# Pooled attention and a residual MLP: casting loads for the first batches, TensorE pools v and k, and a new order of the head

## The chip, the cores and the metric

The kernel runs on one NeuronCore of a Trainium2 chip. TensorE (PE) multiplies matrices, VectorE (DVE) and ScalarE (ACT) work on vectors and may read PSUM, GpSimd (POOL) works on vectors in SBUF and issues the DMAs that cast while they load, SyncE (SP) issues the other DMAs. Each engine runs its instructions in the order in which they were emitted and waits on semaphores where it needs another engine's result. The metric is the time of one execution on the device in microseconds (us), and less is better.

## What is computed

There are 8 batches, 8 heads, 576 positions, 64 features per head.

```
k_p = mean of k over groups of 8 positions     # 72 rows per head
v_p = mean of v over groups of 8 positions
attn = softmax(q @ k_p.T / 8)                  # 576 x 72 per head
x = attn @ v_p, heads side by side             # 8 x 576 x 512
a1 = alpha1 * x + beta1
u = x + lam * (w_tok @ a1)                     # mixes the 576 positions
out = u + lam * (relu((alpha2 * u + beta2) @ w_ch1) @ w_ch2)   # 512 -> 2048 -> 512
```

Inputs and output are fp32; the matmuls take bf16 and fp16.

## The kernel before

The 576 positions of a batch are cut into chunks of 128: four whole ones, and the last 64 positions of two batches share a fifth. The 36 chunks are taken in blocks of four, so there are nine blocks. For each block the kernel runs an MLP: part A (`mlp_A`, L479) multiplies w1 with four chunks of u, 16 steps j of 4 matmuls of 512 columns, each evicted by ScalarE with a relu into a tile `Hj`; part B (`mlp_B`, L497) multiplies `Hj` with w2 in four chunks of four parts.

The attention of a batch b is made of small pieces. `att_F` (L321) turns q to the layout that the scores need, four TensorE transposes and one copy for each pair of heads, or one crossbar transpose on a DMA queue for b > 1. `att_Frem` does so for the last 64 positions. `att_K` (L350, L353) pools k: a matmul with a mask `pool_main` sums positions, after `sum_k` on POOL (L133, L135) has added each four neighbours into one; the result goes to `kpT` in two copies. `att_V` (L364, L366) pools v by three additions on VectorE. `att_S` (L376, L379) makes the scores of one head, three matmuls and two exponentials on ScalarE into a tile `ET`. `att_AV` (L395 to L403) multiplies with v and divides by the sum (the ones stand in a column of the tile `vp1`). `att_X` (L410, L414) multiplies with lam and alpha1 into `xs`. `mix_T` (L444) mixes the positions of one chunk with w_tok, VectorE adds x, and `mix_uT` (L458, L463) turns the result for the MLP. `cast_rem` casts and sums the last 64 positions of q and k.

The order is written out by hand (`manual_schedule`). Ahead of the first MLP step stands a straight list: loads, constants, the attention of batch 0, w_tok's transposes and row sums (L249, L261), four mixes, and the first MLP steps. This is called the head. After it, each block n sorts a list of pieces by a number written beside each: step j of part A has j, parts of B have 16 to 31, and the pieces of the attention of batch n + 1 have numbers between. The function `attention` gives these numbers. An engine's queue has its instructions in that order, DMA issues included: SP's queue holds the loads of q (fp32, batches 0 and 1), k, v and the remainders, the crossbar transposes and the stores; POOL's queue holds the casting loads of w_tok, w1, w2 and, from batch 2 on, q. A tile that a pool hands out again makes the next writer wait for the last reader: `k_raw`, `q_raw`, `v_u` have two buffers each, PSUM's `gp` has six.

In the head of the kernel before, POOL issues the small vectors, then builds the masks by selections, sums k of batch 0, issues w_tok, w1 and w2. VectorE fills the constants in the first 4.7 us, then casts q, waits for beta (L519) and runs on. `keep_warm` (L434) issues matmuls whose result nobody reads.

## Time and profile before

| | before |
|---|---|
| median of 4 runs | 370.61 us (369.58 to 371.78) |
| the profiled execution | 370.36 us |
| its span in the trace | 368.7 us |
| TensorE / VectorE / ScalarE / POOL busy | 94% / 62% / 42% / 22% of the span |
| read from HBM, written to it | 38.04 MB, 9.44 MB |

The profile is one execution. Its page gives for each engine the busy time and the number of instructions, and rows of 40 digits, each the busy share of a fortieth of the span in tenths. PEclk is the clock that the throttle granted to TensorE, in tenths. A row of the stage table is: the stretch in us, its length, busy time and number of instructions of PE, PE's weight loads, DVE, ACT, POOL, then granted clock, busy share of the DMA engines, GB/s. A row of waits is: who waited for whom, total us, times, the longest. A row of the timeline is: start, length, engine, line, operation, out<-in with the form, how many in a row, and in brackets the idle time before it with what ended it.

### The profile page before, as it was taken

The page shows a single profiled execution, that of the slowest core. Times are in us where ns is not written, and L with a number is a line of the kernel's source. Part 1 is how long each engine was busy: PE and PEld are TensorE (multiplying, and loading weights), DVE is VectorE, ACT ScalarE, POOL GpSimd, SP SyncE. Part 2 cuts the span into 40 slices and gives each one's busy share as a digit, 9 for nine tenths or more (in the row PEclk, how much of TensorE's full clock was granted, in tenths as well). Part 3 has the DMA queues.
Part 4 walks back from the last instruction along what each step waited for, and adds up shares of the span by engine and source line. Part 5 has one row for each costly group of instructions (what it writes and reads, how often), then busy time and mean ns, then how long its engine had stood idle before and what let it go on. Part 6 is the DMA issues. An engine that isn't in the chain of part 4 may idle for free.

```text
span 368.7 us, 5783 instructions
## 1 busy us (share of the span) xinstructions
PE 347.8 (94%) x2179; PEld 188.3 (51%) x2179; DVE 228.1 (62%) x459; ACT 156.5 (42%) x317; POOL 82.7 (22%) x94
## 2 busy tenths in 40 slices
PE   2889999789999999999999999999999999999994
PEld 0466656445654565456545654565456545544541
DVE  4697927898876587758775887587748871011011
ACT  1674657316830483048303830384038403703700
POOL 7554143760003500350044003400330000000000
PEclk9999999999999999999999999999999999999999
DMA  8999997937726792788287737864730032011011
GB/s 199 231 186 213 262 196 172 173 46 189 145 72 185 146 164 65 179 183 153 75 212 143 135 75 215 153 132 81 212 80 2 24 92 71 2 57 57 2 57 57
DMA packets 63931, 46.93 MB, mean 127 GB/s; under 512 B 31448, under 2 KB 54044, under 8 KB 63904
## 3 DMA queue, kind: packets, MB, share of 16 engines
q1 hardware_dynamic: 54496, 38.55, 44.7%
q0 software_dynamic: 9408, 8.02, 14.6%
q8 instruction: 17, 0.28, 0.3%
q14 instruction: 10, 0.08, 0.1%
HBM read 38.04 MB, written 9.44 MB: 129 GB/s over the span
## 4 chain that ended last, share of the span: by engine, by line
PE 87%; DVE 7%; DMA 2%; issue 1%; POOL 1%; ACT 0%; POOLq 0%; DVEq 0%
PE ps_h L479 34%; PE ps_ch L497 33%; PE ps_tok L444 12%; PE ps_sc L376 3%; DMA vecs<-in_moe_beta_dram 2%; PE ps_av L395 2%; DVE v_u L364 2%; DVE x_tm L403 2%; DVE xs L410 1%; PE ps_sc L379 1%; DVE vp L366 1%; DVE xs L414 1%; PE ps_uT L463 1%; PE ps_bias L302 1%; DVE rec L401 0%
## 5 line engine op out<-in xcount | busy, mean ns | idle before, releaser
L484 ACT ACTIVATE Hj<-ps_h,bias_cols 128x512 bf16<-128x512 f32 x144 | 98.5, 687 | 154.9 <-PE ps_h L479 153.8
L479 PE MATMUL ps_h<-u_fm,w 128*128 128x512 bf16 (+2 forms) x592 | 137.3, 374 | 0.0
L497 PE MATMUL ps_ch<-w,Hj 128*128 128x512 bf16 x576 | 134.7, 379 | 0.0
L497 PEld LDWEIGHTS <-Hj 128*128 128x128 bf16 x576 | 55.0, 98 | 61.6
L479 PEld LDWEIGHTS <-w 128*128 128x128 bf16 x592 | 62.6, 114 | 45.0 <-issue 0.3
L502 DVE TENSOR_TENSOR u_sb<-u_sb,ps_ch 128x512 f32<-128x512 f32 x36 | 24.6, 687 | 73.8 <-PE ps_ch L497 73.4
L444 PE MATMUL ps_tok<-xs,wtT 128*128 128x512 bf16 (+1 forms) x200 | 49.6, 379 | 3.4 <-DVE xs L410 3.2
L381 ACT ACTIVATE ET<-ps_sc 72x256 f16<-72x256 f32 (+1 forms) x128 | 44.5, 402 | 5.5 <-PE ps_sc L376 4.2
L446 DVE TENSOR_TENSOR u_sb<-x_tm,ps_tok 128x512 f32<-128x512 f32 (+1 forms) x40 | 27.5, 687 | 23.1 <-PE ps_tok L444 23.1
L364 DVE TENSOR_TENSOR v_u<-v_u 72x512 f32<-72x512 f32 x64 | 36.3, 567 | 2.7 <-DMA v_u<-in_v_dram 1.1
L403 DVE TENSOR_TENSOR x_tm<-ps_av,rec 128x320 f32<-128x320 f32 x64 | 31.5, 492 | 2.3
L444 PEld LDWEIGHTS <-wtT 128*128 128x128 bf16 (+1 forms) x200 | 19.1, 98 | 26.5 <-issue 3.7
L118 POOL CAST rem_q<-rem_raw 128x256 bf16<-128x256 f32 x7 | 3.0, 431 | 131.2 <-DMA rem_raw<-in_q_dram 131.2
L448 DVE TENSOR_TENSOR u_bf<-u_sb,al_bc 128x512 bf16<-128x512 f32 (+1 forms) x38 | 29.6, 779 | 1.7 <-DMA u_fm<-u_bf 0.3
L376 PE MATMUL ps_sc<-qT,kpT 128*72 128x256 bf16 x128 | 26.7, 291 | 2.2 <-ACT kpT L358 1.2
L133 POOL TENSOR_TENSOR k_raw<-k_raw 128x512 f32<-128x512 f32 x16 | 20.9, 1304 | 20.9 <-DMA k_raw<-in_k_dram 19.0
L395 PEld LDWEIGHTS <-ET 72*128 72x128 f16 x256 | 16.5, 102 | 12.2 <-DVE v_u L364 0.8
L410 DVE TENSOR_TENSOR xs<-x_tm,lamal_bc 128x512 bf16<-128x512 f32 x29 | 22.0, 759 | 0.9
L135 POOL TENSOR_TENSOR k_bf<-k_raw 128x512 bf16<-128x512 f32 x16 | 22.1, 1382 | 1.3
L401 DVE RECIPROCAL rec<-ps_av 128x5 f32<-128x5 f32 x64 | 12.3, 192 | 15.2 <-PE ps_av L399 14.3
L395 PE MATMUL ps_av<-vp,ET 72*128 72x66 f16 x256 | 18.6, 199 | 0.4 <-ACT ET L381 0.4
L358 DVE CAST kpT<-ps_kp 64x288 bf16<-64x288 f32 x28 | 12.7, 455 | 7.5 <-PE ps_kp L353 7.1
(98 smaller groups left out, 207.4 us busy)
## 6 DMA issues: line engine op xcount, KB each, us to landing
k_raw<-in_k_dram SPq DMA_DIRECT2D x16, 512.0 KB
v_u<-in_v_dram SPq DMA_DIRECT2D x16, 512.0 KB
out_dram<-u_sb SPq DMA_DIRECT2D x32, 256.0 KB
w<-in_moe_w_ch_dram POOLq DMA_DIRECT2D x8, 512.0 KB, 13.7
q_bf<-in_q_dram POOLq DMA_DIRECT2D x12, 256.0 KB, 5.2
q_raw<-in_q_dram SPq DMA_DIRECT2D x4, 512.0 KB
rem_raw<-in_q_dram SPq DMA_DIRECT2D x16, 64.0 KB
rem_raw<-in_k_dram SPq DMA_DIRECT2D x16, 64.0 KB
```

The costliest lines, as they stand in the source:

```text
L364: nc.vector.tensor_tensor(out=t[:, :, 0:n], in0=t[:, :, 0:n], in1=t[:, :, n:2 * n], op=ALU.add)
L376: nc.tensor.matmul(out=ps_sc[0:SPG, 0:256], lhsT=kpT_pool[u][:, half, h % 4, :], rhs=st["qT"][u][:, 2 * (h % 4):2 * (h % 4) + 2, :])
L381: nc.scalar.activation(out=ET[:, n0:n0 + n], in_=ps_sc[0:SPG, 0:n], func=AF.Exp, bias=0.0, scale=0.125)
L395: nc.tensor.matmul(out=av[:, c, :], lhsT=ET[:, m0:m0 + 128], rhs=vp1[:, hh, :])
L403: nc.vector.tensor_tensor(out=x[:, :, dd:dd + D], in0=av[:, :, 0:64], in1=rec.unsqueeze(2).to_broadcast((P, 5, D)), op=ALU.mult)
L410: eng.tensor_tensor(out=xs[:, 0:4, cols], in0=x[:, 0:4, cols], in1=lamal_bc[:, cols].unsqueeze(1).to_broadcast((P, 4, D * (h1 - h0))), op= ...
L444: nc.tensor.matmul(out=ps_tok, lhsT=wtT[0:kk, at, t0:t0 + P], rhs=xs[0:kk, sc, :], start=(sc == 0), stop=(sc == 4))
L446: nc.vector.tensor_tensor(out=s["u"][p0:p1, :], in0=st1[b]["x"][p0:p1, c, :], in1=ps_tok[p0:p1, 0:DM], op=ALU.add)
L448: eng.tensor_tensor(out=s["u_bf"][p0:p1, :], in0=s["u"][p0:p1, :], in1=al2_bc[p0:p1, :], op=ALU.mult)
L479: nc.tensor.matmul(out=ps_h[:, t0:t1], lhsT=w1_of(cc, j), rhs=u_fm[n][:, cc, t0:t1], start=(cc == 0), stop=(cc == 3))
L484: nc.scalar.activation(out=t, in_=ps_h, func=AF.Relu, bias=bias_cols[:, j:j + 1], scale=1.0)
L497: nc.tensor.matmul(out=ps, lhsT=Hj[n, j][:, 128 * m:128 * m + 128], rhs=w2[j // 4][:, j % 4, :], start=(j == 0), stop=(j == NJ - 1))
```

## The change

The head is rewritten, and the attention of batch 1 takes other ways and other numbers.

- q and k of batch 0, v of batches 0 and 1, and q of batch 1 are loaded by POOL's queue with a cast (`load_q_bf`, `load_k16`, `load_v16`). The small vectors are issued by ScalarE. The order in POOL's queue is: q, k of the first four heads, q, k of the others, v, w_tok, w1, q of batch 1, one part of w2, v of batch 1, the rest of w2, with masks, two `att_X` and two `u_bf` between.
- For batch 0, `sum_k` is gone: `att_K` sums over the four neighbours in PSUM by four matmuls instead of one for each head (a fifth column of k, a copy of the first made by VectorE, lets each matmul take two neighbouring columns), and two instead of one for the remainders. Its two copies are on ScalarE and VectorE.
- For batches 0 and 1, v is pooled by TensorE: `first_V`, six matmuls of 256 columns with masks `pool_v`, `pool_vr` for four heads, and two copies.
- q of batch 1 and three chunks of u go through the crossbar on SP's queue.
- `ET` has eight tiles instead of four.
- Several constants (`more_constants`) are filled in the midst of batch 0's attention and not at the start.
- In block 0 the pieces of batch 1 come earlier, during part A, and the four scalings of w2 (2.29 us each in the trace) are spread over the block.

The core of the diff; lines "..." mark what is left out:

```diff
+    def load_k16(b, u):
+        t = work.tile([P, 4, 5, D], BF, tag="k_raw", bufs=2, name="k16")
+        nc.gpsimd.dma_start(out=t[:, :, 0:4].rearrange("p h c d -> p h (c d)"), in_=rows(k, b, u))
+        st1[b]["k"][u] = t
...
+    def load_v16(b, parts=(0, 1, 2)):
+        if 0 in parts:
+            t = work.tile([P, 6, H, D], F16, tag="v_u", bufs=2, name="v16")
...
+                nc.gpsimd.dma_start(
+                    out=main[:, 4 * u:4 * u + 4].rearrange("p h c d -> p h (c d)"),
+                    in_=rows(v, b, u))
...
+    new_batch(0)
+    load_rem(0)
+    load_q_bf(0, 0)
+    load_k16(0, 0)
+    load_vector(1, moe_alpha1)
+    load_vector(0, moe_lam)
...
+    load_q_bf(0, 1)
...
+    load_k16(0, 1)
+    load_v16(0)
...
+    load_wtok()
...
+    def more_constants():
+        nc.vector.memset(ones_bf, 1.0)
+        nc.vector.memset(ones_lo[0:64], 1.0)
+        nc.vector.memset(ones_lo[64:128], 0.0)
+        nc.vector.memset(warm, 0.0)
+        nc.vector.memset(xs_pool[1][0:64, 4, :], 0.0)
+        nc.vector.memset(wtT[:, :, S:640], 0.0)
+        for i, p0 in ((0, 64), (1, 0)):
+            nc.vector.tensor_tensor(out=xs_pool[i][p0:p0 + 1, 4, :], in0=vecs[p0:p0 + 1, 3],
+                                    in1=vecs[p0:p0 + 1, 0], op=ALU.mult)
...
+        n, nr = (1, 1) if b else (4, 2)
+        if not b:
+            nc.vector.tensor_copy(out=st["k"][u][:, :, 4], in_=st["k"][u][:, :, 0])
         for h in range(4):
-            nc.tensor.matmul(out=kp[:, h, 0:64],
-                             lhsT=st["k"][u][:, h].rearrange("p a d -> p (a d)"), rhs=pool_main)
+            for c in range(n):
+                nc.tensor.matmul(
+                    out=kp[:, h, 0:64],
+                    lhsT=st["k"][u][:, h, c:c + 2].rearrange("p a d -> p (a d)"),
+                    rhs=pool_main, start=(c == 0), stop=(c == n - 1))
...
+    def first_V(b, u, copy=nc.vector.tensor_copy):
...
+        for c in range(4):
+            nc.tensor.matmul(out=vp, lhsT=pool_v, rhs=main[:, heads, c], start=(c == 0), stop=False)
+        for c in range(2):
+            nc.tensor.matmul(out=vp, lhsT=pool_vr, rhs=rest[:, heads, c], start=False,
+                             stop=(c == 1))
+        for r in range(2):
+            copy(out=vp1_pool[2 * u + r][:, :, 0:64],
+                 in_=vp[:, 128 * r:128 * r + 128].rearrange("p (h d) -> p h d", h=2))
...
-        if key[0] > 1:
+        if key[0] > 1 or key in ((1, 0), (1, 1), (0, 4)):
             nc.sync.dma_start_transpose(out=u_fm[blk][:, :, 128 * at:128 * at + 128],
...
+    broadcast(0, lam_bc)
     att_F(0, 0)
+    att_F(0, 1, nc.vector.tensor_copy)
+    cast_rem(0, nc.vector)
+    att_K(0, 0, None)
+    att_Frem(0, nc.scalar.copy)
+    att_S(0, 0)
+    att_S(0, 1)
+    att_F(0, 2, nc.vector.tensor_copy)
+    att_F(0, 3, nc.vector.tensor_copy)
+    att_S(0, 2)
+    att_K(0, 1, None)
     nc.vector.tensor_tensor(out=lamal_bc, in0=lamal_bc, in1=lam_bc, op=ALU.mult)
+    more_constants()
+    att_S(0, 3)
+    att_S(0, 4)
+    first_V(0, 0)
+    att_AV(0, 0)
+    att_S(0, 5)
+    att_AV(0, 1)
+    for g in range(4):
+        load_w1(g)
+    att_X(0, 0, 2, nc.gpsimd)
+    first_V(0, 1)
...
+    load_q_bf(1, 0)
+    load_q_bf(1, 1)
+    att_X(0, 2, 4, nc.gpsimd)
+    load_w2(0)
...
+    for u in range(2):
+        load_k(1, u, nc.vector)
+    load_rem(1, behind=nc.vector)
...
     mix_T(0, 1, nc.gpsimd)
+    load_v16(1)
+    for g in range(1, 4):
+        load_w2(g)
...
+        if first:
+            todo.append((3.3, lambda: att_F(b, 0)))
+            todo.append((3.4, lambda: att_F(b, 2)))
+            todo.append((3.5, lambda: cast_rem(b, nc.gpsimd)))
+            todo.append((6.0, lambda: att_Frem(b)))
...
+            todo.append((3.6 + 0.1 * u if first else -0.9 + 1.2 * u,
+                         lambda u=u: sum_k(b, u, nc.gpsimd)))
+            todo.append((6.4 + 3.0 * u if first else 4.1 + 2.0 * u,
+                         lambda u=u: att_K(b, u, nc.scalar.copy if first else nc.vector.tensor_copy)))
+            if first:
+                todo.append((10.2 + 1.4 * u, lambda u=u: first_V(b, u, nc.scalar.copy)))
         for h in range(8):
-            at = 17.0 + 0.9 * h if late else 7.4 + 1.15 * h
-            lag = 1.6 if late else 2.0
+            at = 8.8 + 1.1 * h if first else 7.4 + 1.15 * h
+            lag = 3.0 if first else 2.0
...
-            at = 26.2 + 0.9 * c if late else 19.1 + 1.3 * c
+            at = 21.4 + 1.2 * c if first else 19.1 + 1.3 * c
...
-                todo.append((4.2 + 1.7 * g, lambda g=g: scale_w2(g)))
+                todo.append(((8.0, 13.0, 20.3, 23.9)[g], lambda g=g: scale_w2(g)))
```

## The prediction

> **What bounds the kernel now.** I read the page's shares and 40 slices first, then busy time by stage, then TensorE's waits, then the timeline where stages begin.

> ```profile
> PE 347.8 (94%) x2179; PEld 188.3 (51%) x2179; DVE 228.1 (62%) x459; ACT 156.5 (42%) x317; POOL 82.7 (22%) x94
> ...
> DMA  8999997937726792788287737864730032011011
> ```

> ```profile
> 37.50:56.70 19.20, 18.37 (x168) 11.75 (x168) 11.46 (x11) 12.34 (x24) 6.41 (x6) 1.00 1.06 226
> 56.70:74.70 18.00, 14.41 (x124) 8.52 (x122) 15.31 (x32) 8.35 (x22) 10.89 (x13) 1.00 0.87 163
> 74.70:86.00 11.30, 11.08 (x66) 5.35 (x67) 10.51 (x14) 2.34 (x4) 5.08 (x5) 1.00 0.48 93
> 123.10:160.20 37.10, 37.10 (x231) 19.83 (x229) 27.16 (x54) 15.38 (x32) 8.36 (x10) 1.00 0.70 141
> ```

> ```profile
> PE ps_bc L231 <- DMA vecs<-in_moe_alpha_dram: 7.2, 1, 7.2
> PE ps_tok L444 <- DVE xs L410: 3.2, 2, 2.7
> PE ps_qr L339 <- DVE rem_q L118: 1.4, 1, 1.4
> ```

> ```profile
> 14.71 0.84 PE L376 MATMUL ps_sc<-qT,kpT 128*72 128x256 bf16 x2 [0.48 <-ACT kpT L358]
> ...
> 28.34 0.74 PE L249 MATMUL ps_w<-identity_bf,wt_bf 128*128 128x128 bf16 x5
> ...
> 29.22 0.44 PE L249 MATMUL ps_w<-identity_bf,wt_bf 128*128 128x128 bf16 x5
> ...
> 30.15 1.25 PE L444 MATMUL ps_tok<-xs,wtT 128*128 128x512 bf16 x5 [0.49 <-DVE xs L410]
> ...
> 37.52 0.81 PE L479 MATMUL ps_h<-u_fm,w 128*128 128x384 bf16 x4
> ...
> 85.94 4.26 PE L479 MATMUL ps_h<-u_fm,w 128*128 128x512 bf16 x19
> ```

> From 86 us on TensorE has no gap (37.10 busy of 37.10 in one whole block), and the change leaves that list of work as it is. So all that can change is the start of block 1's first matmul, 85.94. Before it lie two stages: the head, to the first mixing matmul (30.15) and the first MLP matmul (37.52, 7.4 later), and block 0, 48.4 us, of which TensorE idles 0.83 + 3.59 + 0.22 = 4.6. The DMA row is at 9 for the first 64 us: the head is fed by full queues.

> **The loads.** Removed: q, k, v of the first batch as fp32 on SP, and with them q's casts (0.7 on VectorE, 1.1 on ScalarE). Added: as bf16/f16 casts on POOL. In the trace's packet records an fp32 load passes at 340 packets of 1024 B per us (512 packets: 1.5 us); the cast loads of later batches (q_bf) at 380 of 512 B (1.35 us), 2.2 to 2.9 us after POOL begins to issue, and about 1 us more until a waiter runs. Halved bytes thus save a tenth, not half. [...]
> With POOL's first issue at 0.8: q0 usable 5.8, k0 7.1, q1 8.5, k1 9.8, v0 11.2, v1 13.0, w_tok 16.9 (37 packets/us: 3.5 us, and the rest 0.4), w1 19.5 to 27.3 (2.6 each). Before, w_tok ends near 21 and w1 near 31. Each POOL issue costs 0.6 to 0.8 us; q1, k1 and v are issued between the mask selections and still queue behind flowing data, so that is hidden. [...] The small vectors move to ScalarE's queue: one landing took 7.2 us to TensorE's first work, now some 3.5; hidden behind q0.

> **The head, step by step.** F transposes: 8 at 0.107 = 0.9, to 6.7. VectorE then copies qT (0.55), casts rem_q (0.28) and rem_k (two pieces, some 0.4) and fills k's fifth column (bounds 0.1 and 0.3 by the rem_q row; 0.15): 8.1. K's fourth matmul waits for that column; everything on TensorE is queued behind it. The rest of K, 13 of 64 columns at 0.054 and the remainder, ends 9.0 (K now costs 1.0 instead of 0.4 us, twice). kpT: VectorE's half waits for ScalarE's half by their common tile, so 0.4 + 0.4 still: 10.0. The first scores are complete at 10.4 against some 15.2: 4.8 gained, since no POOL sums (2.5) and no DMA of beta through VectorE's queue (the 1.4 wait at L339) are ahead of them.
> Then S1 0.5, F 0.9, S2 0.5, K1 1.0 (with its column): 13.4; kpT of the second half 14.5. Here VectorE's own list comes: lamal 0.68, six memsets (rows 0.11 to 0.27: 1.2), two xs rows 1.3 (L519 took 1.8 with POOL beside; 0.65 each is the lower end, and POOL is idle here), first_V's two copies (no row; half the width of kpT's 0.45 to all of it, 0.2 to 0.45; 0.25): 18.2. TensorE has S3, S4 and V (1.0 + 1.3) done at 15.8 and waits 2.3 us in AV0, everything else queued behind. This is a new wait: the memsets lay under the loads before.
> From 18.2 VectorE leads: eight AV pairs at 0.62 (L401 and L403 by their starts), two copies 0.5, a wait for the second V 0.6, X(4,6) 0.8 and 0.5 for POOL's X beside it (L410 took 0.68 alone, 0.93 and more beside POOL), memsets 0.2, X(6,8) 0.7: 8.3, the mix at 26.5. If TensorE is still at its slow rate, its list from AV0 (8 AV 0.28, 3 S 0.5, V 1.3, broadcast 1.2, 10 transposes 1.1) is 7.4 plus 1.7 for the last AV's X and some VectorE lag: 27.7. Against it stands v's old sums, 6 to 7 us on VectorE in 14.8 to 26.5, gone.
> Which rate? The two L249 rows above are one and the same work at 0.107 and 0.056 us per transpose: TensorE doubled at 29.0, while PEclk says 1.00 throughout. [...] I take 27.0: 3.1 gained. The 7.4 to the first MLP matmul stay (same lists; w1's first part landed by 19.5): 34.4.

> **Block 0.** TensorE loses 18 transposes of q (some 1.1) and three u tiles (0.2 each, now on the crossbar), gains two V (0.7 each): -0.3. Of the 4.6 us idle, 2.7 is L444 waiting for xs behind VectorE and POOL, both full in 56.7 to 74.7 (v sums, k sums, X); the v sums (1.4 x 4) and kpT copies leave VectorE, scores come during the A part, and X has room. What is late next: ScalarE. Between A8 and A15 it has 8 Hj 5.5, 16 ET some 6, kpT and vp 1.8: 13.3 against TensorE's 12.5 (eight A 6.9, S 2.4, V 1.4, K and bias 1.0, AV 0.8), so 1 to 2 us of waits for PSUM. POOL: two u_bf (to 32), six issues (4.5), rem 1.1, sums 2.6 each: k ready at 40.4 and 43, needed by K at 34.4 + 9.5 = 43.9 (four A's 3.7, bias 0.6, three A's 2.6, w_tok's last part with its wait 1.4, the mix of chunk 4 1.2). q's crossbar transposes (1.3 each on SP) wait for q of the second batch (31 to 33), needed near 47; behind them on SP stand only loads for the third batch; v 38, needed 49; w2 40 to 46, needed from 57. All are covered by 3 us or more, and if one is not, TensorE stops in the A part with everything behind it, us for us. The four extra ET memsets (0.11 each) lie under the first load; the extra ET buffers spare waits that the waits of before do not show, so I count nothing. Left idle 2.0: block 43.8 - 0.3 + 2.0 = 45.5, 2.9 gained.

> **Sum.** The profiled run took 370.36 (span 368.7 and 1.7 around it; the median is 370.61): 370.36 - 3.1 - 2.9 = 364.4.

> **Rivals.** (1) As summed, 364.4, own range 361 to 366.5 (fast clock early and no idle in block 0: 370.4 - 4.5 - 4.6): 0.60. (2) Only one half comes: VectorE's chain or ScalarE in block 0 eats it. For: both run at 95% there. Time 370.4 - 3.1 = 367.3: 0.20. (3) It does not do what it says: POOL's first load is as late as the vectors' 6.3 us to landing (2 us), VectorE's list adds 1, block 0 idles as before: 370: 0.12. (4) Slower: the clock gate. The new waits at K, K1 and AV0 keep the rate slow past the mix. From the mix at 27.7 to the end of the first A's TensorE has 11 us of fast work; every us of it done slow costs 1 us more. It decides once the release comes 5 us or more after the mix (2.4 + 2.9 gained are used up); all 11 give 370.4 - 5.3 + 11 = 376. Against it: the mix itself is dense 512-wide work. 0.08.

> A measurement tells 0.5% (1.9 us) from no change. Faster: (1) and (2), 0.80; same 0.12; slower 0.08. The range 361 to 369 takes in (1) and (2).

> **What would show it.** Scores begin near 10; AV0 waits some 2 us for VectorE; first mix near 27, first MLP matmul near 34.4, block 1 near 80; L444's 2.7 wait gone. Wrong if q0 lands after 7.5, if K waits for POOL in block 0, or if a 128-wide transpose still takes 0.107 after the mix.

## The result, and the profile after

| | before | after |
|---|---|---|
| median, in the comparison of the two | 371.25 us (64 runs) | 371.28 us (43 runs, 368.94 to 374.24) |
| the profiled execution | 370.36 us | 369.31 us |
| its span | 368.7 us | 367.6 us |
| start of the first mix, the first MLP matmul, block 1, us | 30.15, 37.52, 85.94 | 29.77, 37.46, 84.57 |

The ratio is 1.0012, 95% interval 0.9997 to 1.0026: no change. Forecast were 364.4 us and a range of 361 to 369, so the time lies outside it. (Here and below a ratio is to the kernel before and leaves out executions that lie over 1.5% above the fastest of their kernel, among them 14 of 22 in r2, 9 of 14 in s1, 9 of 22 in s3 and 13 of 22 in s4, while medians are over all.)

The page of after, busy time and the clock's row of 40 slices:

```profile
PE 350.6 (95%) x2201; PEld 189.7 (52%) x2201; DVE 213.2 (58%) x449; ACT 151.3 (41%) x312; POOL 88.7 (24%) x97
...
PEclk9968999999999999999999999999999999999998
```

VectorE lost 15 us of work, as meant. But TensorE is busy for 2.8 us longer than before, and PEclk has a 6 and an 8 in the third and fourth slice. Before, it was 9 in every slice, but that row says nothing of the time ahead of 29.0 us: the clock's record in the trace begins at 29.0 before and at 13.4 in after, and up to then the row reads full while a 128-wide transpose took 0.107 us (0.056 behind 29.0 in before). So before, the head ran at the slow rate up to 29.0. The stage table shows what after did:

```profile
15.00:20.00 5.00, 2.14 (x23) 1.49 (x24) 4.42 (x14) 1.53 (x6) 0.00 (x0) 1.00 1.18 203
20.00:25.00 5.00, 5.00 (x32) 2.79 (x29) 2.84 (x9) 1.95 (x7) 3.88 (x5) 0.53 1.25 206
25.00:30.00 5.00, 4.59 (x51) 4.23 (x51) 4.27 (x15) 3.82 (x8) 1.52 (x3) 0.50 1.35 208
...
37.46:57.00 19.54, 18.23 (x177) 12.06 (x177) 3.95 (x5) 14.01 (x34) 7.41 (x9) 1.00 1.08 223
57.00:74.70 17.70, 17.70 (x121) 9.51 (x120) 14.81 (x25) 5.68 (x14) 15.02 (x13) 1.00 0.44 75
74.70:84.57 9.87, 7.55 (x41) 3.52 (x40) 8.65 (x9) 1.17 (x2) 6.12 (x4) 1.00 0.47 69
```

In the first row TensorE works 2.14 us of 5 and VectorE 4.42; in the next two TensorE is full or nearly so, at half its clock. In block 0 (last three rows) the middle stretch has no idle time any more, but 1.31 and 2.32 us remain at its two ends. TensorE's waits name the causes:

```profile
PE ps_av L455 <- DVE vp L417: 2.6, 1, 2.6
PE ps_uT L523 <- DVE u_bf L508: 2.3, 1, 2.3
...
PE ps_rs L296 <- ACT wtT L287: 1.3, 1, 1.3
```

The wait of 2.7 us in block 0 for xs at L444 (L504 now) is gone. AV0 (`att_AV` of head 0) waits 2.6 us for vp, the pooled v, from VectorE, near the 2.3 forecast. And on the timeline:

```profile
10.95 0.92 PE L436 MATMUL ps_sc<-qT,kpT 128*72 128x256 bf16 x2 [0.26 <-ACT kpT L402]
...
19.31 0.30 PE L455 MATMUL ps_av<-vp,ET 72*128 72x66 f16 x4 [2.60 <-DVE vp L417]
...
28.62 0.74 PE L284 MATMUL ps_w<-identity_bf,wt_bf 128*128 128x128 bf16 x5
29.77 1.58 PE L504 MATMUL ps_tok<-xs,wtT 128*128 128x512 bf16 x5 [0.41 <-DVE xs L470]
...
37.46 0.81 PE L539 MATMUL ps_h<-u_fm,w 128*128 128x384 bf16 x4
...
84.57 1.67 PE L539 MATMUL ps_h<-u_fm,w 128*128 128x512 bf16 x7
```

The scores begin 3.8 us earlier than before (14.71), and nothing is left of it at the first MLP matmul (37.46 against 37.52). Block 0 takes 47.1 us instead of 48.4. So two questions: who ate the head's gain, and why is block 0 only 1.3 us shorter, where 2.9 was forecast? From block 1's start to the end of the time, the profiled runs of both kernels and of the experiments take 284.2 to 285.0 us, so the start of block 1 tells the time. Three runs have the very head of after (after itself, r4, t1): their first MLP matmul comes at 37.46, 37.38 and 37.91, so a few tenths between two heads mean nothing.

### The profile page after: what moved, and what is told of

The parts are those of the page before. It is cut to its first block, busy times and chain, and to the rows that moved or that the text cites. A ratio compares the mean times of both kernels' runs of the same rounds, so it can differ in the third digit from the quotient of the medians.

```text
span 367.6 us, 5843 instructions
## 1 busy us (share of the span) xinstructions
PE 350.6 (95%) x2201; PEld 189.7 (52%) x2201; DVE 213.2 (58%) x449; ACT 151.3 (41%) x312; POOL 88.7 (24%) x97
## 3 DMA queue, kind: packets, MB, share of 16 engines
HBM read 38.04 MB, written 9.44 MB: 129 GB/s over the span
## 4 chain that ended last, share of the span: by engine, by line
PE 87%; DVE 6%; DMA 2%; issue 1%; SPq 1%; ACT 1%; DVEq 0%
PE ps_h L539 33%; PE ps_ch L557 32%; PE ps_tok L504 10%; PE ps_sc L436 4%; PE ps_av L455 2%; DMA rem_raw<-in_k_dram 2%; PE ps_sc L439 1%; DVE u_bf L508 1%; SPq L351 1%; DVE w L327 1%; PE ps_kp L389 1%; DVE u_sb L506 1%; DVE x_tm L463 1%; DMA rem_qT<-rem_q 1%; DVE xs L470 1%
## 5 line engine op out<-in xcount | busy, mean ns | idle before, releaser
L562 DVE TENSOR_TENSOR u_sb<-u_sb,ps_ch 128x512 f32<-128x512 f32 x36 | 24.7, 687 | 75.3 <-PE ps_ch L557 74.8
L504 PE MATMUL ps_tok<-xs,wtT 128*128 128x512 bf16 (+1 forms) x200 | 49.7, 381 | 0.4 <-DVE xs L470 0.4
L506 DVE TENSOR_TENSOR u_sb<-x_tm,ps_tok 128x512 f32<-128x512 f32 (+1 forms) x40 | 27.4, 685 | 26.5 <-PE ps_tok L504 26.4
L142 POOL CAST rem_q<-rem_raw 128x256 bf16<-128x256 f32 x7 | 5.0, 721 | 129.6 <-DMA rem_raw<-in_q_dram 129.6
L504 PEld LDWEIGHTS <-wtT 128*128 128x128 bf16 (+1 forms) x200 | 19.4, 98 | 24.3 <-issue 1.0
L461 DVE RECIPROCAL rec<-ps_av 128x5 f32<-128x5 f32 x64 | 12.3, 192 | 25.8 <-PE ps_av L459 25.0
L424 DVE TENSOR_TENSOR v_u<-v_u 72x512 f32<-72x512 f32 (+1 forms) x48 | 26.5, 552 | 1.2
L155 POOL TENSOR_TENSOR k_raw<-k_raw 128x512 f32<-128x512 f32 x14 | 18.9, 1349 | 15.8 <-DMA k_raw<-in_k_dram 15.8
L157 POOL TENSOR_TENSOR k_bf<-k_raw 128x512 bf16<-128x512 f32 x14 | 21.3, 1523 | 1.1
L470 DVE TENSOR_TENSOR xs<-x_tm,lamal_bc 128x512 bf16<-128x512 f32 x27 | 18.7, 692 | 0.9
L402 DVE CAST kpT<-ps_kp 64x288 bf16<-64x288 f32 x26 | 11.8, 456 | 9.1 <-PE ps_kp L395 6.1
```

Of the source, the lines that this page charges most:

```text
L424: nc.vector.tensor_tensor(out=t[:, :, 0:n], in0=t[:, :, 0:n], in1=t[:, :, n:2 * n], op=ALU.add)
L504: nc.tensor.matmul(out=ps_tok, lhsT=wtT[0:kk, at, t0:t0 + P], rhs=xs[0:kk, sc, :], start=(sc == 0), stop=(sc == 4))
L506: nc.vector.tensor_tensor(out=s["u"][p0:p1, :], in0=st1[b]["x"][p0:p1, c, :], in1=ps_tok[p0:p1, 0:DM], op=ALU.add)
L562: nc.vector.tensor_tensor(out=u, in0=u, in1=ps, op=ALU.add)
```

## The experiments

Theory: VectorE's list ahead of vp makes TensorE wait at AV0, and because of this wait the granted clock falls again (from 1.00 to 0.50 at 20.3 in after), which costs 4 to 5 us (an estimate). Rival: VectorE's own chain sets the first mix, whatever the clock.

### The memsets first (r1)

```diff
+    nc.vector.memset(ones_bf, 1.0)
+    nc.vector.memset(ones_lo[0:64], 1.0)
...
     nc.vector.tensor_reduce(out=pool_rem, in_=pool_each, op=ALU.max, axis=AX.X)
...
     def more_constants():
-        nc.vector.memset(ones_bf, 1.0)
-        nc.vector.memset(ones_lo[0:64], 1.0)
...
```

> The six memsets of more_constants (16.21 to 17.5 in the trace of after) are filled before pool_rem, where VectorE stood idle from 3.75 to 5.23; the two xs rows (1.39) stay ahead of vp. The wait at AV0 falls from 2.6 to some 1.3 us. Theory 1 (the wait lets TensorE fall back to its slow clock, which then costs 4 to 5 us to the mix): if 1.3 us are too short for the fall, the granted clock reads 1.00 in 20 to 30 us, the first mix comes near 25.5 instead of 29.77, and the time falls by 3.5 to 5 us; if they are long enough, only the 1.3 us come back. Rival (VectorE's own chain from vp to the last X sets the mix, whatever the clock): the mix at 28.5, 1.2 us less.

Measured: 369.89 us, ratio 0.9965 (0.9941 to 0.9989). AV0 waits 1.3 us and the clock stays at 1.00 to 27.5. The first mix comes at 27.54, between the two numbers, but now with a wait of 2.9 us for xs before it; then the clock falls, and the first MLP matmul is at 36.55. Behind the wait of 1.3 us the clock does not fall here, behind the one of 2.9 it does (0.50 from 27.6 to 31.0), and what was taken off one wait came back as another.

### Nothing ahead of vp (r2)

```diff
         for i, p0 in ((0, 64), (1, 0)):
-            nc.vector.tensor_tensor(out=xs_pool[i][p0:p0 + 1, 4, :], in0=vecs[p0:p0 + 1, 3],
+            nc.gpsimd.tensor_tensor(out=xs_pool[i][p0:p0 + 1, 4, :], in0=vecs[p0:p0 + 1, 3],
...
-    more_constants()
     att_S(0, 3)
...
         load_w1(g)
+    more_constants()
     att_X(0, 0, 2, nc.gpsimd)
```

(in addition to the edit of r1)

> As the run with early memsets, and the two xs rows go to GpSimd, which is idle from 13.6 to 21.1 us; nothing but lamal (0.69) is left on VectorE ahead of vp, and AV0 waits 0 to 0.3 us. Theory 1: clock 1.00 from 13 us on, no fall in 20 to 30; first mix at 24.5 to 25.5, first MLP matmul near 32.5 (37.46 in after), time 4 to 5 us below after. Rival (VectorE's chain): the 2.6 us come back and no more, mix at 27.2, and the slow clock need not go. A third case: the loads of batch 1 (k, w1) do not come earlier, and block 0 gives part of it back in waits for DMA: then the first MLP matmul is early but block 1 is not (84.57 in after).

Measured: 377.32 us over all executions, 368.44 the fastest; ratio 0.9993 (0.9965 to 1.0022). AV0 still waits 0.6 us. The head did nearly as the rival said (27.2): mix at 26.76 after a wait of 3.0 us, clock 0.50 from 27.1 to 30.5, first MLP matmul at 35.79. The rest is the third case, and worse than it was put: in block 0 TensorE stood 5.8 us for the crossbar's rem_qT, the turned last 64 positions of q:

```profile
54.69 0.24 PE L439 MATMUL ps_sc<-rem_qT,kpT 128*72 128x64 bf16 x1 [5.78 <-DMA rem_qT<-rem_q]
```

In after it does not wait for it in block 0 at all: its only wait of the kind, 0.4 us, is for batch 2, at 92.66 in block 1.

### The wait filled (r3)

```diff
     first_V(0, 0)
+    keep_warm(10)
     att_AV(0, 0)
```

> The wait at AV0 stays as long as it is, but TensorE runs ten matmuls of 512 columns in it whose result nobody reads (0.216 us each at the fast clock, 2.2 us). Nothing is computed sooner. Theory 1: the clock does not fall in 20 to 30 us, the transposes of w_tok take 0.056 us instead of 0.107, the first mix comes 1.5 to 2.5 us sooner than in after (29.77), being bound by VectorE then, and the time is 1.5 to 2.5 us less. Rival (VectorE's chain sets the mix whatever the clock): mix at 29.5 to 29.8, no change in time, or up to 0.5 us more.

Measured: 372.16 us, ratio 1.0003 (0.9979 to 1.0027). TensorE's timeline and stages:

```profile
17.20 2.33 PE L494 MATMUL ps_warm<-warm,identity_bf 128*128 128x512 bf16 x10 [0.22 <-DVE warm L256]
...
25.45 0.44 PE L284 MATMUL ps_w<-identity_bf,wt_bf 128*128 128x128 bf16 x5
28.81 1.40 PE L504 MATMUL ps_tok<-xs,wtT 128*128 128x512 bf16 x5 [2.93 <-DVE xs L470]
31.07 4.46 PE L504 MATMUL ps_tok<-xs,wtT 128*128 128x512 bf16 x15
```

```profile
20.00:25.00 5.00, 4.80 (x69) 3.57 (x66) 4.24 (x14) 3.69 (x10) 3.80 (x5) 1.00 1.24 205
...
30.00:35.00 5.00, 5.00 (x25) 2.67 (x24) 1.90 (x3) 0.52 (x2) 2.09 (x2) 0.68 1.06 309
```

The idle wait had cost the clock: with ten matmuls in it that nobody reads, it stays at 1.00 up to 29.8 and the transposes of w_tok take 0.44 instead of 0.74 us for five. But the mix gains only 1.0 us (28.81), because it waits 2.9 us for xs; and behind this wait the clock falls in its turn (0.68 in 30 to 35), so that the fifteen matmuls of the other mixes take 4.46 instead of the 3.41 of before and the first MLP matmul is at 37.83, no earlier than in after. Neither theory alone is right: the two causes stand in series.

### Both waits filled (s1)

```diff
     att_X(0, 6, 8)
+    keep_warm(13)
     mix_T(0, 0, nc.gpsimd)
```

(in addition to the edit of r3)

> As the run with the filled wait, and 13 more matmuls without a reader (2.8 us) fill the wait of 2.9 us that stood there before the first mix. Nothing is computed sooner than in that run. Theory (two causes in series: VectorE's chain sets the first mix, near 28.8 whatever the clock, and any 3.41 us window of TensorE that is mostly idle costs the next 3.41 us at half rate, 1.7 us of dense work): the clock stays at 1.00 through the mix, from the first mix to the first MLP matmul 7.4 us pass instead of 9.0, the first MLP matmul comes at 36.2 instead of 37.8, and the time is 1.5 us below the run with one wait filled. Rival (what follows the mix is bound by VectorE's additions and u_bf, not by the rate): the 9.0 stay, no change.

Measured: the head as foretold:

```profile
28.82 1.24 PE L504 MATMUL ps_tok<-xs,wtT 128*128 128x512 bf16 x5
...
36.17 0.81 PE L539 MATMUL ps_h<-u_fm,w 128*128 128x384 bf16 x4
```

Between after and s1 only matmuls that nobody reads differ, and TensorE stays at the fast rate through the head (five transposes of w_tok in 0.44 to 0.45 us, the first mix in 1.24). The slow clock's share of the head is thus 37.46 - 36.17 = 1.3 us, and not the 4 to 5 of my theory. The mix at 28.8 is VectorE's, whose timeline in s1 has:

```profile
19.06 0.48 DVE L417 CAST vp<-ps_v 72x128 f16<-72x128 f32 x2
...
24.78 1.45 DVE L470 TENSOR_TENSOR xs<-x_tm,lamal_bc 128x512 bf16<-128x512 f32 x1
26.15 0.53 DVE L474 TENSOR_TENSOR xs<-x_tm,lamal_bc 64x128 bf16<-64x128 f32 x1
```

From the end of the first vp copies (19.54) to the mix 9.3 us pass. One X (`att_X`; X(4,6) is that of heads 4 and 5) takes 1.45 and 0.53 beside POOL's, the other, X(6,8), 0.69 for its first piece alone. In after itself the path was another: at half the clock TensorE was late with the fifth AV, which stands behind two broadcasts, and VectorE waited for it:

```profile
22.87 2.07 PE L266 MATMUL ps_bc<-vecs,ones_row 1*128 1x512 f32 x2
```

```profile
25.37 0.20 DVE L461 RECIPROCAL rec<-ps_av 128x5 f32<-128x5 f32 x1 [1.67 <-PE ps_av L459]
```

Its X(4,6) then ran alone (0.69 and 0.28). The time of s1 did not follow (376.84 us over all, 369.03 the fastest, ratio 0.9987, 0.9952 to 1.0022): the profiled run stands 7.3 us at rem_qT.

### The remainder on TensorE (s2), and the mix filled too (s3)

```diff
-            todo.append((6.0, lambda: att_Frem(b)))
+            todo.append((6.0, lambda: att_Frem(b, nc.scalar.copy)))
```

s2 is r2 with this edit; s3 is s2 with `keep_warm(13)` before the first mix.

> As the run with vp first, and the remainder of q of batch 1 is turned by TensorE (two transposes and a copy) instead of the crossbar. Theory: the 5.8 us that TensorE waited for rem_qT in block 0 came from SP's queue, which moves only some 14 GB/s while the w2 loads flow; without it the waits at rem_qT are gone, block 1 starts 1.5 us sooner than in after (first MLP matmul at 35.8 instead of 37.46, block 0 still 47 us) and the profiled time is near 367.7. Rival: the other crossbar transposes (qT) are late just so, and the scores wait for them instead: 372 to 377 again.

> As the run with the remainder on TensorE, and the wait of 3 us before the first mix is filled with 13 matmuls without a reader. Theory: the clock stays at 1.00, the first mix comes at 26.8 as there, the first MLP matmul at 34.2 instead of 35.8 (the forecast had 34.4), and the time is 1.5 us below that run, near 366. Rival (the rate does not matter there): 35.8, no change.

s2: 369.76 us, ratio 0.9954 (0.9929 to 0.9979); first MLP matmul at 35.69, the wait for rem_qT of batch 1 gone. Its profiled run, 369.49, misses the expected 367.7, and the clock has most of that: it fell once more behind the wait of 2.3 us for u_bf at the end of block 0, from whose end to block 1 6.1 us pass instead of the 4.6 of after. s3 reached in the head what the prediction had (27.0 and 34.4):

```profile
26.73 1.24 PE L504 MATMUL ps_tok<-xs,wtT 128*128 128x512 bf16 x5 [0.18 <-DVE xs L470]
...
34.08 0.81 PE L539 MATMUL ps_h<-u_fm,w 128*128 128x384 bf16 x4
```

and yet took 370.79 us (ratio 0.9948, 0.9922 to 0.9973): the other crossbar transposes are late now. Its waits, SP's timeline, and a stage:

```profile
PE ps_sc L436 <- DMA qT<-q_bf: 3.2, 2, 2.2
```

```profile
31.82 12.04 SPq L351 DMA_TRANSPOSE qT<-q_bf  x2
```

```profile
43.00:47.00 4.00, 3.95 (x41) 2.39 (x40) 3.65 (x3) 2.84 (x7) 1.85 (x2) 1.00 1.97 49
```

The two transposes hold SP's queue for 12.0 us (3.3 in after), and while the loads in POOL's queue run beside them the DMA engines are busy but move 49 GB/s, where some 200 were usual in the head. In after the transposes are issued 1.7 us ahead of the loads of v and 3.8 ahead of the last three parts of w2 (33.34, 35.01, 37.15); in s3, whose head is earlier, 0.2 behind v and 2.0 ahead of w2 (31.82, 31.62, 33.77).

### Block 0 (r4)

```diff
-            todo.append((5.4, lambda: mix_T(0, 4)))
-            todo.append((4.6, lambda: (setup_wtok(4, nc.scalar.copy), setup_rowsum(4))))
+            todo.append((6.2, lambda: mix_T(0, 4)))
+            todo.append((5.1, lambda: setup_rowsum(4)))
+            todo.append((4.6, lambda: setup_wtok(4, nc.vector.tensor_copy)))
...
-                todo.append(((8.0, 13.0, 20.3, 23.9)[g], lambda g=g: scale_w2(g)))
+                todo.append(((8.0, 13.0, 20.3, 11.5)[g], lambda g=g: scale_w2(g)))
```

What it undoes, on VectorE's timeline of after:

```profile
67.87 2.29 DVE L327 TENSOR_TENSOR w<-w,lam_bc 128x2048 bf16<-128x2048 bf16 x1
...
74.94 3.35 DVE L327 TENSOR_TENSOR w<-w,lam_bc 128x2048 bf16<-128x2048 bf16 x1
...
78.92 1.04 DVE L508 TENSOR_TENSOR u_bf<-u_sb,al_bc 128x512 bf16<-128x512 f32 x1
```

The fourth scaling lies right ahead of the addition and the u_bf that TensorE needs, and takes 3.35 instead of 2.29 us; it is beside POOL's sums for batch 2, one of which takes 3.19 us then and 1.60 just before.

> Only block 0 is changed: the fourth scaling of w2 goes from 23.9 to 11.5 (VectorE idle from 50.3 to 56.6 in after), w_tok's last part is copied by VectorE, its row sum comes one step later. Theory: the waits of 2.3 us (u_bf behind the scaling, which took 3.35 instead of 2.29 beside GpSimd) and 1.3 us (row sum behind ScalarE) are gone, block 0 takes 43.6 to 44.5 us instead of 47.1, and the time is 3 to 3.5 us less. Rival: another wait takes their place (the fourth part of w2 lands only near 51.6, and VectorE's AV work queues behind its scaling; u_bf beside GpSimd's sums takes 1.04 instead of 0.7): 1 to 2 us of it come back.

Measured: 366.36 us (366.08 to 367.05), ratio 0.9877 (0.9856 to 0.9898). The theory holds, with 4.9 us from the median of after to that of r4 instead of 3 to 3.5. In the waits and on the timeline of r4:

```profile
PE ps_uT L523 <- DVE u_bf L508: 0.4, 1, 0.4
```

```profile
37.38 0.81 PE L539 MATMUL ps_h<-u_fm,w 128*128 128x384 bf16 x4
...
81.23 4.48 PE L539 MATMUL ps_h<-u_fm,w 128*128 128x512 bf16 x20
```

Block 0 takes 43.85 us, 3.3 less than in after. The head is unchanged, clock included (0.54 and 0.50 in 20 to 30), and the runs lie within 1 us where those of after lie within 5.3. How much each of its edits gives was not taken apart; by the waits of after it is 2.3 and 1.3 us.

### The wait in block 0 filled (t1)

```diff
+            todo.append((26.7, lambda: keep_warm(9)))
```

> As after, and nine matmuls without a reader (1.95 us) fill the wait of 2.3 us in which TensorE stands in block 0 for u_bf behind the fourth scaling of w2 (77.7 to 80.0). Nothing is computed sooner. Theory: in most executions of after that wait takes most of one 3.41 us window and makes the next one slow (1.7 us), which is why its median (371.28) lies 2 us above its profiled run (369.31); with the wait filled the runs lie together between 368.9 and 369.9. Rival (the spread of after has another cause, in the head or the loads): median 371 and a spread of 5 us as before.

Measured: 370.07 us, ratio 0.9968 (0.995 to 0.9986). Nine matmuls at 77.99 (2.10 us) fill the wait, block 0 is as long as before (37.91 to 85.05), and the median falls by 1.2 us. So in these runs that wait costs more than its length, by way of the clock. Two other records agree. In r3 the same wait is followed by a fall of the clock, and from its end to block 1 6.24 us pass (80.40 to 86.64), where after, whose profiled run has no fall there, takes 4.55. And of the 43 executions of after, the 16 with a mean granted clock of 0.969 to 0.975 took 372.7 to 374.2 us, the 13 with 0.981 to 0.986 took 368.9 to 370.4; in t1 none is below 0.976, in r4 none below 0.981. The spread only shrinks from 5.3 to 3.9 us, so the theory explains most of it and not all.

### All together (s4), and two ways around the crossbar (u1, u2)

s4 is s3 with the edit of r4.

> As the run with the mix filled, and block 0 with the edit of the block-0 run (fourth scaling of w2 early, w_tok's last part on VectorE, its row sum later). Theory (head and block 0 add up): first MLP matmul at 34.2, block 0 in 43.5 to 44.5 us, time 361.5 to 363.5, below both kernels. Rival (with an earlier head block 0 meets its loads: k of batch 1 by POOL's sums, w2, the crossbar): 364 to 366.

370.77 us over all executions, 364.95 the fastest, ratio 0.9894 (0.9862 to 0.9926): the rival, and more. The profiled run stands 10.8 us at qT, the turned q of batch 1:

```profile
PE ps_sc L436 <- DMA qT<-q_bf: 10.8, 1, 10.8
```

Two kernels, each s4 with one more edit, ask why; u1 turns q of batch 1 on TensorE, u2 keeps the crossbar and issues three loads of w2 after POOL's sums of k, and with them changes the order of two scalings:

```diff
-        if b:
+        if b > 1:
...
-            todo.append((3.3, lambda: att_F(b, 0)))
-            todo.append((3.4, lambda: att_F(b, 2)))
+            for hp in range(4):
+                todo.append((5.3 + 0.5 * hp, lambda hp=hp: att_F(b, hp, nc.vector.tensor_copy)))
```

```diff
     load_v16(1)
-    for g in range(1, 4):
-        load_w2(g)
...
+                todo.append((3.8, lambda g=g: load_w2(g)))
...
-                todo.append(((8.0, 13.0, 20.3, 11.5)[g], lambda g=g: scale_w2(g)))
+                todo.append(((8.0, 11.5, 20.3, 13.0)[g], lambda g=g: scale_w2(g)))
```

> As the run with all edits, and q of batch 1 is turned by TensorE as in before (sixteen transposes, 0.9 us, and four copies on VectorE, which is idle there) instead of the crossbar. Theory: the 10.8 us that TensorE waited for qT come from the crossbar transposes on SP's queue; without them no DMA wait is left in block 0 and all runs lie together, near 363.5 (first MLP matmul 34.3, block 0 in 44.5 to 45.5). Rival (q itself lands late, behind the loads in POOL's queue): TensorE then waits for q_bf at the transposes, and the time stays between 366 and 374.

> As the run with all edits, crossbar kept, but the loads of the last three parts of w2 are issued by GpSimd after its sums of k (near 42 us instead of 33 to 36), and their scalings follow in the order they land. Theory: the crossbar's packets on SP's queue are held up by the w2 loads on the other queue (14 GB/s beside 195); with these later, qT and rem_qT land by 45, TensorE does not wait for them, and the time is 362 to 363.5 in all runs. Rival (the crossbar's late q has another cause): the waits for qT stay, 366 to 374; or w2 is now late: TensorE waits near 57 to 62 for the scaled w2, 1 to 4 us.

u1: 363.69 us (362.81 to 364.72), ratio 0.9781 (0.9758 to 0.9804); the wait for qT is gone, and one of 1.3 us for POOL's sums of k stands in block 0. u2: 363.95 us (363.23 to 368.44), ratio 0.9813 (0.9773 to 0.9853), no wait for qT, and on SP's timeline and in the stages:

```profile
31.11 5.67 SPq L351 DMA_TRANSPOSE qT<-q_bf  x2
```

```profile
44.00:48.00 4.00, 3.95 (x43) 2.63 (x42) 3.45 (x3) 3.66 (x8) 0.80 (x2) 1.00 0.99 183
```

Both theories hold: with the early head the stall needs the crossbar and the w2 loads together, and without either the median is 7.3 to 7.6 us below that of after. Why the two clash in the DMA engines, no run tells.

### vp on ScalarE (u4)

```diff
-    first_V(0, 0)
+    first_V(0, 0, nc.scalar.copy)
...
-    first_V(0, 1)
+    first_V(0, 1, nc.scalar.copy)
```

(in addition to the edits of u2, and with nine matmuls instead of thirteen before the mix)

> As the run with w2 later, and vp of batch 0 is copied by ScalarE, idle there, instead of VectorE; the filling before the mix is cut from 13 to 9 matmuls. Theory (VectorE's chain from vp to the last X sets the first mix): it is 1.0 us shorter, the first mix comes at 25.8 to 26.2 and the time is 0.7 to 1 us below the run with w2 later. Rival (ScalarE's exponentials, behind which the copies queue, delay vp and AV as much as VectorE is relieved): the mix stays at 26.7 to 27.1.

367.37 us, ratio 0.9909 (0.9875 to 0.9943), 3.4 us more than u2. The rival's number: the mix stays at 26.99, but not quite for its reason. X(4,6) took 1.58 us beside POOL's, and VectorE waited three times for TensorE's AV (0.4 to 0.9 each). In block 0 TensorE waited 2.2 us for x_tm (the attention's x), which in u2 it does not: VectorE had stood 3.0 us for a part of w2, and its scaling (2.29 us from 57.44) lay ahead of the AV work. That part landed at 57.4, in u2 at 55.1. It is the late w2 that the rival of u2 named, so moving these loads has a price near it; why they landed later here stays open.

## Why the prediction was wrong

By its own sum the forecast missed 6.9 us: 371.28 against 364.4. The profiled run accounts for 4.9: the head 3.06 (37.46 for 34.4), block 0 1.6 (47.1 for 45.5), the rest 0.3 (block 1 has the new wait of 0.4 for batch 2's rem_qT). The median lies another 2.0 above the profiled run, of which t1 gives back 1.2.

**The loads**: the first was nearly right, the next were late. q0 was usable at 6.3 (5.8), since POOL's first issue came at 1.32 and not at 0.8; but k0 landed at 8.5 (7.1), q1 at 9.9 (8.5) and k1 at 11.3 (9.8). No TensorE wait names k1. Nor are the bytes that a load reads halved: by their pages both kernels read 38.04 MB from HBM, so a cast load still reads fp32. And a term was missing: VectorE waited 0.64 us, up to 8.77, for the load of k's remainder on SP before it could fill k's fifth column, which was ready at 9.4 and not at 8.1. The first scores were complete at 11.9 (10.4).

**VectorE's list before AV0**: the wait was right (2.60 us, 2.3 forecast), its end 1.2 us late (19.4, 18.2 forecast). The list began 1.0 late, at 15.54 behind a kpT forecast for 14.5, and took 3.9 us instead of 3.7.

**First mix at 26.5 to 27.7**: this step failed; the mix came at 29.77. The sum has two branches, one for each rate of TensorE. After ran the slow one, forecast 27.7. AV0 began 1.1 us late (above), and from AV0 to the mix 10.5 us passed instead of 9.5: the two broadcasts were put at 1.2 us, which is their price at the fast rate (1.12 in s1), and took 2.07, as at the slow rate in the trace of before, and what VectorE had left behind the last AV took 2.6 us, where 1.7 and some lag were put. The fast branch, forecast 26.5, is s1: the mix came at 28.8, because the list was 1.2 late and from the vp copies to the mix 9.3 us passed instead of 8.3; X(4,6) beside POOL was put at 0.8 plus 0.5 and took 2.0, and the wait for the fifth AV behind the broadcasts (0.5) was not counted.

Under both lies the second half of the failed step: "Which rate?" asked only when TensorE gets fast, and not what the new wait does to a clock that is already at 1.00. The 27.0 lies between the two branches; no run had shown when the new head would get fast, so it was my estimate. In after the clock was at 1.00 from 13.4 us on and fell to 0.50 at 20.3: the 2.3 us wait was entered as time alone, and behind it the rate was also halved, for 10.2 us. Of the 3.06 us by which the head missed, 1.8 are VectorE's (28.8 for 27.0) and 1.3 the clock's (s1), and as much again was lost where a wait stood elsewhere (t1: 1.2). My fourth rival had the slow clock, but as one that gets fast late and not as one that falls again, and at 0.08. With VectorE's list elsewhere and the wait before the mix filled, 26.73 and 34.08 came true (s3), so the early head was there to be had.

**Block 0, left idle 2.0**: 3.6, and the culprit was misnamed. ScalarE gave 1.3, so "next late" had the engine, but at the row sum and not in waits for PSUM; 2.3 was the fourth scaling, 2.29 us long by the row, moved by this change right ahead of u_bf, and 3.35 long there, beside POOL's sums. The prediction listed the scalings as spread over the block and did not ask who queues behind each. r4 shows the size: 3.3 us of block 0 and 4.9 of the median. The terms for TensorE's work (43.5) were right: 43.49 us busy in after, 43.44 of 43.85 in r4.

**"All are covered by 3 us or more"**: right for q of the four chunks (landed by 42.2, needed at 50.2), wrong for the remainder. Issued at 39.21, rem_qT landed at 49.05 by the trace's semaphores and was used at 50.42, so 1.4 us covered it, in r4 none that can be seen (49.01, used at 49.05). What I took for cover was the late head: with 1.3 to 3.4 us less of it TensorE stood 3 to 11 us (r2, s1, s3, s4), because POOL's loads and the transposes hamper each other (49 GB/s in all from 43 to 47 in s3; no such stall in u1 and u2, where one or the other is away). The three-us estimate used the transposes' own 1.3 us on SP and no contention.

**Rivals**: it ended nearest to the third (370: "VectorE's list adds 1, block 0 idles as before"), though by other sums. The low end of my own range was a slip: it gave the head 4.5 us, where its earliest mix, 26.5, gives 3.7. None of the three signs of being wrong appeared (q0 landed at 6.3, K did not wait for POOL in block 0, transposes after the mix were fast), so they watched the wrong steps; scores, AV0's wait and L444 came as forecast, and that did not save the sum.

## What to carry to other kernels

A wait that a change puts on TensorE is to be entered twice: its length, and the clock that it may take away afterwards (here 2.6 us, and then 10.2 us at 0.50); where TensorE would stand anyway, a few matmuls that nobody reads can hold the clock (ten in r3: 1.00 up to 29.8; with thirteen more in s1: 1.3 us of the head). When a piece of work is moved to another place on an engine's queue, ask what stands right behind it there. And the cover of a transfer that was measured with a late start is gone when the start comes earlier: count it from the new start, with what else flows then.

## What the runs showed of the hardware

| kernel | TensorE idle, us | longest part in one step, us | behind it |
|---|---|---|---|
| before | 72.0 to 74.8 | 1.4 | clock does not fall |
| after | 16.7 to 19.3 | 2.5 | 0.50 from 20.3, for 10.24 us |
| after | 77.7 to 80.0 | 1.7 | clock does not fall |
| r3 | 78.1 to 80.4 | 2.3 | 20 matmuls of 512 columns from 80.63 take 6.17 us (4.48 in r1) |
| r3 | 25.9 to 28.8 | 2.5 | 0.50 from 29.8, for 3.41 us |
| r4 | 17.2 to 19.2 | 1.9 | 0.50 from 20.4, for 10.24 us |
| r1 | 76.8 to 79.1 | 1.9 | 20 matmuls of 512 columns from 79.36 take 4.48 us |
| r1 | 16.8 to 18.1 | 0.8 | clock does not fall |
| r1 | 24.6 to 27.5 | 2.9 | 0.50 from 27.6, for 3.41 us |

The length of the wait alone does not decide: 2.7 us cut in halves left the clock alone (before), 2.3 us did so in after and did not in r3. In this table the waits with 2.3 us or more in one step were followed by a fall, those with 1.7 or less were not, and of the two with 1.9 one was. Over the 199 steps at 1.00 in the records of before and after, the three in which TensorE was busy for 0.38 or less of the step (after from 16.84, and the last one at 1.00 of each kernel) were followed by 0.50, the others, with 0.49 or more, were not. The fall came up to 1.2 us after the wait had ended (r4: 19.2 and 20.4).

After a fall the clock was back at 1.00 in 3.41 us where the dense mixes ran (r1, r3), and only in 10.24 us behind AV0 in after, where the short scores, AV products and broadcasts ran, though TensorE was busy for 1.00, 1.00 and 0.88 of the three steps. In u2 the rate fell without a long wait: five transposes of w_tok take 0.45 us at 21.39 and 0.74 at 22.66, and two broadcasts from one row (1.12 us from 19.58) stand ahead of it; in s1 the same two, from 21.98, were not followed by a fall (0.45 and 0.44 for five transposes). That a busy TensorE is not enough is shown; what decides is not.
